# Agent attention and a gated feed-forward: attention matmuls moved to even steps, scores in one piece

## The chip, the core and the metric

The kernel runs on one core of a Trainium2 chip. The core has a matrix engine (TensorE, PE in the profile, with its weight loads as PEld), three elementwise engines (VectorE or DVE, ScalarE or ACT, GpSimd or POOL) and SyncE (SP), which here only issues DMAs. Each engine works through its own instruction queue in order and waits on semaphores of the others. The metric is the device time of one execution, in microseconds (us).

## The reference

```
q, k, v: (4, 12480, 128)   agents: (4, 49, 128)   w_in: (128, 2048)   w_out: (2048, 128)
sm(a, b)  = softmax(a @ b.T / sqrt(128))
agent_v   = sm(agents, k) @ v            # 49 x 128 per batch, over all 12480 keys
x         = sm(q, agents) @ agent_v      # 12480 x 128 per batch
h         = x @ w_in
out       = (h * sigmoid(1.702 * h)) @ w_out
```

All in float32; the kernel reaches the precision by splitting operands into parts that TensorE multiplies one after the other.

## The kernel before

The kernel folds `agent_v` into `w_in`: for each batch it computes the 49 x 2048 product `agent_v @ w_in` once (`weights_0`, `weights_1`, `weights_part`, into the tiles `wh` and `wq`), so that a query's softmax row over 49 agents is multiplied straight into the hidden layer.

Queries are worked in 52 groups of 960 tokens (13 for each of the 4 batches), in two halves of 480 columns. For each group the 2048 hidden units are 16 **steps** of 128. The main loop, `two_steps(t)`, takes two steps at a time, so 416 rounds. TensorE's work in a round is always the same:

- `up`: four matmuls of 128 rows (L407) and then **the quad** (L410), four matmuls with 19 rows each, placed in four row groups of the array. They leave four banks `ph` in PSUM;
- two calls of `down`, six matmuls of 480 columns each (L445), which add the hidden units of the steps `t - 4` and `t - 3` to `po`.

Between them ScalarE applies the gelu from `ph` to `g` (L420), `high` rounds it to `gh` (by a DMA that POOL issues, or by ACT or DVE, depending on the step), and DVE computes the rest, `gl = g - gh` (`low`, L435).

The attention work of the following groups and of the next batch is slipped in between. A table `at` maps a step number to the jobs that are issued there. **Where a job lands in a round depends on the parity of its step**: `jobs(t)`, the even step, is called behind the quad and ahead of the first `down`; `jobs(t + 1)`, the odd step, is called in `second`, between the two `down`s. `pe_steps` is the set of steps that already hold TensorE work; `pe_step(t)` returns the first free one from `t` on.

The jobs that matter here:

- **Scores** (`scores`, L186): a group of 960 keys or queries is split into three bf16 parts (`split`: four DVE pieces at L173 and L175 that write `rest`; pieces 0 and 1 belong to the first 480 tokens, 2 and 3 to the others). Then 48 small matmuls (49 columns, bf16) produce 8 tiles of scores in one PSUM bank, 24 of them (c = 0) for the first half of the tokens and 24 (c = 1) for the other. A query group has c = 0 at step 12 of its 16 and c = 1 at step 13; a key group has them at the first two free steps from a rule on.
- **`key_store`** (L228): ACT copies the bank of key scores to `score` in SBUF; then DVE updates the running maximum from the bank (`running_max`, L225).
- **`query_shift`** (L350, L352): DVE subtracts each query's maximum; it needs the whole bank.
- **`key_values`** (L284): eight matmuls of 258 columns, `exp(score)` times values, after `value_pair` (L279, L280) has written the one buffer `v_pair`.
- `key_max_1`, `key_max_2`, `weights_1` (L311 to L313), `weights_part` (L330): a few matmuls for each batch; `query_pairs` (L379, then L389 and L391) transposes the softmax rows at step 4.

SP issues the loads (`key_load`, `query_load`, `value_load`) in the order of the steps. There are two PSUM banks (`ps_m`) for all the attention work, two buffers for `rest`, one for a query group's load.

Of the kernel before, what the change touches and what calls it, by code (L numbers as in the profile page):

```python
# [18 lines left out]
TB = 120  # L19
KB = 8  # L20
# [7 lines left out]
Q_AT = 12  # L28
E_AT = 0
P_AT = 4  # L30
S_AT = 8
K_AT = 3
V_AT = (6, 11)
V_LAST = 5
R = 30
FIRST_WORDS = 1
FIRST_UP = 2
# [6 lines left out]
def kernel(  # L44
# [11 lines left out]
    B, C, N = qT.shape  # L56
    A = agT.shape[2]
    F = w_in.shape[1] // 2
    NF = F // P
    NG = N // GT  # L60
    NKG = N // (TB * KB)
# [28 lines left out]
    for i in range(2):  # L90
        t = const.tile([P, KB, P], F32R, name=f"e_pair{i}")
# [14 lines left out]
    score = const.tile([P, NKG * KB, A], F32, name="score")  # L106
# [59 lines left out]
    def split(t):  # L166
        r = work.tile([P, GT + PAD], F32, name="rest", tag="rest")
        nc.gpsimd.memset(t[:, GT:], 0.0)

        def piece(i):  # L170
            s = slice(0, CH + PAD) if i < 2 else slice(CH + PAD, GT + PAD)
            if i % 2 == 0:
                nc.vector.tensor_sub(out=r[:, s], in0=t[:, s], in1=halves(t)[0][:, s])  # L173
            else:
                nc.vector.tensor_sub(out=halves(r)[1][:, s], in0=r[:, s], in1=halves(r)[0][:, s])  # L175

        return (halves(t)[0], halves(r)[0], halves(r)[1]), piece

    def scores(b, parts, ps, c):
        x0, x1, x2 = parts  # L180
        for j in range(c * KB // 2, (c + 1) * KB // 2):
            t = slice(j * TB, j * TB + P)
            o = ps[:, j * A : (j + 1) * A]
            products = [(x0, 0), (x0, 1), (x0, 2), (x1, 0), (x1, 1), (x2, 0)]
            for i, (x, y) in enumerate(products):
                nc.tensor.matmul(  # L186
                    out=o,
                    lhsT=x[:, t],
                    rhs=ag_part[:, b, y, :],
                    start=(i == 0),  # L190
                    stop=(i == len(products) - 1),
                )

    def score_bank():
        ps = ps_m.tile([P, 512], F32, name="ps_m")
        return ps, ps[:TB, : KB * A].rearrange("p (j a) -> p j a", a=A)
# [24 lines left out]
    def running_max(g, s):  # L221
        if g == 0:
            nc.vector.tensor_copy(out=run_max[:TB], in_=s)
        else:
            nc.vector.tensor_tensor(out=run_max[:TB], in0=s, in1=run_max[:TB], op=ALU.max)  # L225

    def key_store(g, s):
        nc.scalar.copy(out=score[:TB, g * KB : (g + 1) * KB, :], in_=s)  # L228
        running_max(g, s)

    def key_max_0(d):
        mx = work.tile([P, A], F32, name="mx", bufs=1)
        nc.vector.tensor_reduce(out=mx[:TB], in_=run_max[:TB].rearrange("p j a -> p a j"), axis=AX.X, op=ALU.max)
        d["mx"] = mx
# [28 lines left out]
    def key_shift(g, sub):  # L263
        sc = score[:TB, g * KB : (g + 1) * KB, :]
        sub(out=sc, in0=sc, in1=max_b[:TB].unsqueeze(1).broadcast_to([TB, KB, A]), op=ALU.subtract)  # L265
# [5 lines left out]
    def key_pair(g):  # L271
        sc = score[:TB, g * KB : (g + 1) * KB, :]
        ep = e_pair[g % 2]
        nc.vector.tensor_copy(out=ep[:TB, :, 0:A], in_=sc)
        nc.vector.tensor_sub(out=ep[:TB, :, H : H + A], in0=sc, in1=ep[:TB, :, 0:A].bitcast(F32))
# [67 lines left out]
    def query_load(b, g):  # L343
        t = loads.tile([P, GT + PAD], F32, name="qt", tag="qt", bufs=1)
        nc.sync.dma_start(out=t[:, 0:GT], in_=qT[b, :, g * GT : (g + 1) * GT])
        return t

    def query_shift(s):
        m = work.tile([P, KB], F32, name="m")
        nc.vector.tensor_reduce(out=m[:TB], in_=s, axis=AX.X, op=ALU.max)  # L350
        sd = e_sb[:TB, :, 0:A]
        nc.vector.tensor_tensor(  # L352
            out=sd, in0=s, in1=m[:TB].unsqueeze(2).broadcast_to([TB, KB, A]), op=ALU.subtract
        )
        return sd
# [118 lines left out]
    def do_key_load(b, g):  # L474
        if b < B and g < NKG:
            kts[b, g] = key_load(b, g)
# [5 lines left out]
    def do_query_load(n):  # L482
        if n < B * NG:
            qts[n] = query_load(*divmod(n, NG))

    def do_key_split(b, g, i):
        if i == 0:
            k_parts[b, g], pieces[b, g] = split(kts.pop((b, g)))
        pieces[b, g](i)
# [7 lines left out]
    def do_key_scores(b, g, c):  # L497
        if c == 0:
            banks[b, g] = score_bank()
        scores(b, k_parts[b, g], banks[b, g][0], c)  # L500

    def do_key_store(b, g):
        key_store(g, banks.pop((b, g))[1])

    def do_key_values(b, g):
        sums[b, g] = key_values(g)
# [6 lines left out]
    def do_query_scores(n, c):  # L513
        if n < B * NG:
            if c == 0:
                banks[n] = score_bank()
            scores(n // NG, q_parts[n], banks[n][0], c)

    def do_query_shift(n):
        if n < B * NG:  # L520
            scored[n] = query_shift(banks.pop(n)[1])
# [94 lines left out]
    steps = B * NG * NF  # L616
    per_batch = NG * NF
    at = {}
    pe_steps = {n * NF + f for n in range(B * NG) for f in (Q_AT, Q_AT + 1, P_AT)}

    def put(t, fn):
        at.setdefault(t, []).append(fn)


    def pe_step(t):
        while t in pe_steps:
            t += 1
        pe_steps.add(t)
        return t
# [7 lines left out]
    for b in range(B - 1):  # L637
        s0 = b * per_batch
        done = s0
        for k in range(NKG):  # L640
            t = pe_step(s0 + (11 + 5 * k if b == 0 else K_AT + 11 * k // 2))
            t1 = pe_step(t + 1)
            put(t - 13 if b else max(t - 13, 0), lambda b=b, k=k: do_key_load(b + 1, k))
            begin = max(t - 4, done + 1)
            for i in range(4):
                put(min(begin + i, t - 1 if i < 2 else t1 - 1), lambda b=b, k=k, i=i: do_key_split(b + 1, k, i))
            done = t1
            put(t, lambda b=b, k=k: do_key_scores(b + 1, k, 0))
            put(t1, lambda b=b, k=k: do_key_scores(b + 1, k, 1))
            put(t1 + 1, lambda b=b, k=k: do_key_store(b + 1, k))  # L650
        mx = {}
        put(t1 + 2, lambda mx=mx: key_max_0(mx))
        t = pe_step(t1 + 3)
        put(t, lambda mx=mx: key_max_1(mx))
        t = pe_step(t + 2)
        put(t, lambda mx=mx: key_max_2(mx))
        shift = t + 1

        g0 = (shift + 1 - s0 - E_AT + NF - 1) // NF
        for k in range(NKG):  # L660
            slot = s0 + (g0 + k // 2) * NF + E_AT
            exps.setdefault(slot, []).append(k)
            last = k == NKG - 1
            t = slot + (V_LAST if last else V_AT[k % 2])
            put(min(shift + 3 * k, slot - 1), lambda k=k: key_shift(k, nc.vector.tensor_tensor))
            put(t - 16, lambda b=b, k=k: do_value_load(b + 1, k))
            put(t - 4, lambda b=b, k=k: value_pair(vts.pop((b + 1, k))))
            put(slot + 3 - last, lambda k=k: key_pair(k))
            assert t not in pe_steps
            put(t, lambda b=b, k=k: do_key_values(b + 1, k))  # L670
            put(t + 1, lambda b=b, k=k: do_key_sum(b + 1, k))
        w = {}
        put(t + 2, lambda b=b, w=w: weights_0(accs.pop(b + 1), w))
        t = pe_step(t + 3)
        put(t, lambda w=w: weights_1(w))
        for c in range(F // 512):
            t = pe_step(t + (3 if c else 1))
            assert t < s0 + per_batch + 4 * c - 5, (b, shift - s0, g0, t - s0)
            put(t, lambda b=b, w=w, c=c: weights_part(b + 1, w, c))
    for n in range(B * NG):  # L680
        s0 = n * NF
        if n:
            put(s0 + E_AT, lambda n=n: do_query_exp(n + 1))
            if s0 + E_AT in exps:
                ks = exps[s0 + E_AT]
                put(s0 + E_AT, lambda ks=ks: key_exp(ks[0], len(ks)))
            put(s0 + E_AT + 2, lambda n=n: do_query_sums(n + 1))
            put(s0 + E_AT + 2, lambda n=n: do_query_softmax(n + 1))
        put(s0 + P_AT, lambda n=n: do_query_pairs(n + 1))
        for i in range(4):  # L690
            put(s0 + S_AT + i, lambda n=n, i=i: do_query_split(n + 2, i))
        for c in range(2):
            put(s0 + Q_AT + c, lambda n=n, c=c: do_query_scores(n + 2, c))
        put(s0 + Q_AT + 2, lambda n=n: do_query_load(n + 3))
        put(s0 + Q_AT + 2, lambda n=n: do_query_shift(n + 2))


    E = mybir.EngineType
    g = {}
# [98 lines left out]
```

## Time and profile before

| | |
|---|---|
| median of 3 runs | 2039.23 us (2039.01 to 2040.26) |
| the profiled execution's own time | 2040.92 us |
| its span, from the first to the last instruction | 2039.1 us |
| VectorE busy | 1576.9 us (77%) |
| ScalarE busy | 1440.2 us (71%) |
| GpSimd busy | 281.4 us (14%) |
| mean share of the 16 DMA engines, by slices | 3 to 9 tenths, mostly 5 |
| granted clock of TensorE | 0.988 on average; full speed in all but the first slices |

The profiled execution is 1.69 us above the median of the runs, and its span 1.82 us below its own time. The page's busy time of TensorE counts instructions whose modelled ends overlap; what a piece of its work costs is read from the starts of what follows, in the chain of waits or in the timeline.

### The profile page before, as it was taken

To read this page: it belongs to the slowest core of one execution; us is meant where nothing else is said; L and a number is where in the kernel's file an instruction comes from. 1 tells how busy PE (TensorE), PEld (TensorE's weight loads), DVE (VectorE), ACT (ScalarE), POOL (GpSimd) and SP (SyncE) were. 2 spreads that over 40 slices of the span, in tenths; PEclk is the share of its full clock that TensorE was granted. 3 is DMA by queue.
4 is the path that set the end of the run, shared out by engine and by line. 5 is a ranking of instruction groups with operands and counts; after the bars stand their busy time and mean duration, and the time that the engine had idled before them with its cause. 6 is when DMAs were issued, how large, how long until landed. Compare 5 with 4: busy or idle time off the path is not lost.

```text
span 2039.1 us, 36417 instructions
## 1 busy us (share of the span) xinstructions
PE 1992.4 (98%) x13688; PEld 1525.2 (75%) x13688; DVE 1576.9 (77%) x2025; ACT 1440.2 (71%) x2457; POOL 281.4 (14%) x594
## 2 busy tenths in 40 slices
PE   8789999999999999999999999999999999999999
PEld 7567777777777777777777777777777777777776
DVE  4788888888777879888777888888877776767665
ACT  3256677677776777777776677777777877777775
POOL 3011111111111111111111111111111111111111
PEclk9799999999999999999999999999999999999999
DMA  9645556565455565565555555566545545455443
GB/s 252 180 157 182 180 181 184 172 190 174 159 170 174 181 191 181 173 190 175 170 172 171 180 190 175 170 191 174 170 164 161 178 156 170 155 171 165 161 157 134
DMA packets 129444, 356.00 MB, mean 175 GB/s; under 512 B 15696, under 2 KB 48688, under 8 KB 129268
## 3 DMA queue, kind: packets, MB, share of 16 engines
q0 software_dynamic: 67520, 230.22, 34.4%
q1 hardware_dynamic: 61748, 123.46, 20.9%
q8 instruction: 108, 1.77, 0.4%
q14 instruction: 68, 0.56, 0.1%
HBM read 80.97 MB, written 25.56 MB: 52 GB/s over the span
## 4 chain that ended last, share of the span: by engine, by line
PE 89%; DVE 5%; ACT 2%; DMA 2%; issue 1%; POOL 1%; SPq 0%; ACTq 0%; POOLq 0%; DVEq 0%
PE po L445 53%; PE ph L407 17%; PE ph L410 8%; PE ps_m L186 6%; PE ps_m L284 2%; DVE gl L435 1%; DMA gh<-g 1%; PE ps_m L379 1%; PE ps_m L209 1%; ACT g L420 1%; PE ps_m L330 1%; DVE rest L173 1%; DVE rest L175 1%; POOL score L265 1%; DMA words<-w_in 0%
## 5 line engine op out<-in xcount | busy, mean ns | idle before, releaser
L420 ACT ACTIVATE g<-ph 128x480 f32<-128x480 f32 x1664 | 816.6, 577 | 494.4 <-PE ph L410 489.3
L435 DVE TENSOR_TENSOR gl<-g,gh 128x960 fp32r<-128x960 f32 x832 | 941.3, 1153 | 192.5 <-DMA gh<-g 101.9
L445 PE MATMUL po<-gh,wo_h 128*128 128x480 f32 x1664 | 551.7, 413 | 1.9 <-DMA gh<-g 1.9
L445 PE MATMUL po<-gl,wo_h 128*128 128x480 f32 x1664 | 502.1, 383 | 4.9 <-DVE gl L435 4.3
L445 PE MATMUL po<-gh,wo_l 128*128 128x480 f32 x1664 | 500.2, 382 | 0.0
L426 POOL DMA_DIRECT2D gh<-g x468 | 252.0, 538 | 1689.9 <-ACT g L420 1129.2
L445 PEld LDWEIGHTS po<-gl,wo_h 128*128 128x128 f32 x1664 | 311.6, 189 | 63.0 <-DVE gl L435 14.9
L445 PEld LDWEIGHTS po<-gh,wo_l 128*128 128x128 f32 x1664 | 314.0, 189 | 49.8
L445 PEld LDWEIGHTS po<-gh,wo_h 128*128 128x128 f32 x1664 | 273.2, 189 | 85.4 <-issue 64.8
L407 PE MATMUL ph<-sa,wh 128*128 128x480 f32 x832 | 319.8, 384 | 4.8 <-ACT g L420 3.3
L407 PE MATMUL ph<-sb,wh 128*128 128x480 f32 x832 | 321.6, 386 | 0.0
L430 ACT CAST gh<-g 128x960 fp32r<-128x960 f32 x312 | 311.8, 999 | 9.0
L410 PE MATMUL ph<-rq,wq 19*128 19x480 f32 x1664 | 205.2, 481 | 0.0
L407 PEld LDWEIGHTS ph<-sa,wh 128*128 128x128 f32 x832 | 157.4, 189 | 37.4 <-ACT g L420 11.0
L407 PEld LDWEIGHTS ph<-sb,wh 128*128 128x128 f32 x832 | 157.2, 189 | 35.4 <-ACT g L420 11.6
L410 PEld LDWEIGHTS ph<-rq,wq 19*128 19x128 f32 x1664 | 80.0, 182 | 137.0 <-issue 136.5
L186 PE MATMUL ps_m<-ag_part,rest 128*128 128x49 bf16 x2184 | 130.3, 185 | 6.6 <-DVE rest L175 6.4
L175 DVE TENSOR_TENSOR rest<-rest 128x480 bf16<-128x480 f32 (+1 forms) x182 | 129.8, 719 | 0.4
L186 PEld LDWEIGHTS <-rest 128*128 128x128 bf16 x2184 | 109.4, 97 | 8.4 <-DVE rest L175 7.8
L225 DVE TENSOR_TENSOR run_max<-ps_m,run_max 120x392 f32<-120x392 f32 x36 | 20.4, 567 | 79.3 <-ACT score L228 79.1
L186 PEld LDWEIGHTS <-qt 128*128 128x128 bf16 x1248 | 61.3, 98 | 25.1 <-issue 25.0
L186 PE MATMUL ps_m<-ag_part,qt 128*128 128x49 bf16 x1248 | 74.6, 186 | 0.0
(97 smaller groups left out, 1326.8 us busy)
## 6 DMA issues: line engine op xcount, KB each, us to landing
gh<-g POOLq DMA_DIRECT2D x468, 480.0 KB, 3.6
kt<-kT SPq DMA_DIRECT2D x52, 480.0 KB
qt<-qT SPq DMA_DIRECT2D x52, 480.0 KB
vt<-v SPq DMA_DIRECT2D x52, 480.0 KB
outT<-o SPq DMA_DIRECT2D x104, 240.0 KB
rq<-sa SPq DMA_DIRECT2D x104, 35.6 KB
rq<-sb SPq DMA_DIRECT2D x104, 35.6 KB
sa<-sa SPq DMA_DIRECT2D x104, 28.1 KB
```

Source lines behind the costliest of these rows:

```text
L173: nc.vector.tensor_sub(out=r[:, s], in0=t[:, s], in1=halves(t)[0][:, s])
L175: nc.vector.tensor_sub(out=halves(r)[1][:, s], in0=r[:, s], in1=halves(r)[0][:, s])
L186: nc.tensor.matmul(out=o, lhsT=x[:, t], rhs=ag_part[:, b, y, :], start=(i == 0), stop=(i == len(products) - 1),)
L225: nc.vector.tensor_tensor(out=run_max[:TB], in0=s, in1=run_max[:TB], op=ALU.max)
L284: nc.tensor.matmul(out=ps[:, : 2 * C + 2], lhsT=e_pair[g % 2][:TB, j, :], rhs=v_pair[:TB, j, :], start=(first and j == 0), stop=(last and ...
L407: nc.tensor.matmul(out=ph[k][:, :CH], lhsT=wh[:, cols[i]], rhs=pairs[c], start=True, stop=False)
L410: nc.tensor.matmul(out=ph[k][:, :CH], lhsT=wq[r, cols[i]], rhs=rq[r], start=False, stop=True, tile_position=(k * 32, 0),)
L420: nc.scalar.activation(out=gs[i][:, c, :], in_=ph[k][:, :CH], func=AF.Gelu_apprx_sigmoid)
L426: nc.gpsimd.dma_start(out=gh, in_=g)
L430: nc.scalar.copy(out=gh, in_=g)
L435: nc.vector.tensor_sub(out=gl, in0=g, in1=gh.bitcast(F32))
L445: nc.tensor.matmul(out=po[c][:, :CH], lhsT=lhsT[:, f, :], rhs=rhs[:, c, :], start=(begin and first), stop=(end and last),)
```

## The change

All TensorE jobs of the attention are put at even steps, so behind a quad. `pe_step` returns only even steps. The two halves of a group's scores stand at the same step, one behind the other. A key group's steps are two written lists (`K_FIRST` for the keys that are scored during batch 0, `K_AT` for later batches), asserted to be free; the four split pieces all stand ahead of that step. The second value group of a slot moves from step 11 to step 10. The query's load and shift move from step 14 to step 13. The running maximum moves out of `key_store` to the step after it, and reads the stored `score` in SBUF and not the PSUM bank.

```diff
-K_AT = 3
-V_AT = (6, 11)
-V_LAST = 5
+K_FIRST = (10, 16, 22, 26, 32, 38, 42, 48, 54, 58, 62, 66, 70)
+K_AT = (6, 10, 16, 22, 26, 32, 38, 42, 48, 54, 58, 64, 70)
+V_AT = (6, 10)
...
         nc.scalar.copy(out=score[:TB, g * KB : (g + 1) * KB, :], in_=s)
-        running_max(g, s)
...
-    pe_steps = {n * NF + f for n in range(B * NG) for f in (Q_AT, Q_AT + 1, P_AT)}
+    pe_steps = {n * NF + f for n in range(B * NG) for f in (Q_AT, P_AT)}
...
-        while t in pe_steps:
+        while t % 2 or t in pe_steps:
...
-            t = pe_step(s0 + (11 + 5 * k if b == 0 else K_AT + 11 * k // 2))
-            t1 = pe_step(t + 1)
+            t = s0 + (K_AT if b else K_FIRST)[k]
+            assert pe_step(t) == t
...
-                put(min(begin + i, t - 1 if i < 2 else t1 - 1), lambda b=b, k=k, i=i: do_key_split(b + 1, k, i))
-            done = t1
-            put(t, lambda b=b, k=k: do_key_scores(b + 1, k, 0))
-            put(t1, lambda b=b, k=k: do_key_scores(b + 1, k, 1))
-            put(t1 + 1, lambda b=b, k=k: do_key_store(b + 1, k))
+                put(min(begin + i, t - 1), lambda b=b, k=k, i=i: do_key_split(b + 1, k, i))
+            done = t
+            for c in range(2):
+                put(t, lambda b=b, k=k, c=c: do_key_scores(b + 1, k, c))
+            put(t + 1, lambda b=b, k=k: do_key_store(b + 1, k))
+            put(t + 2, lambda k=k: running_max(k, score[:TB, k * KB : (k + 1) * KB, :]))
...
-            last = k == NKG - 1
-            t = slot + (V_LAST if last else V_AT[k % 2])
+            t = slot + V_AT[k % 2]
...
-            put(slot + 3 - last, lambda k=k: key_pair(k))
+            put(slot + 3, lambda k=k: key_pair(k))
...
-            put(s0 + Q_AT + c, lambda n=n, c=c: do_query_scores(n + 2, c))
-        put(s0 + Q_AT + 2, lambda n=n: do_query_load(n + 3))
-        put(s0 + Q_AT + 2, lambda n=n: do_query_shift(n + 2))
+            put(s0 + Q_AT, lambda n=n, c=c: do_query_scores(n + 2, c))
+        put(s0 + Q_AT + 1, lambda n=n: do_query_load(n + 3))
+        put(s0 + Q_AT + 1, lambda n=n: do_query_shift(n + 2))
```

Line numbers of the changed kernel behind `key_store` are one below those of before.

The first place is TensorE at steps 12 and 13 of a query group. Before, the last score matmul of the first half (from `rest`) is followed by a whole `down` of six, and then the second half begins (from `qt`):

```order
L186 LDWEIGHTS rest
L186 MATMUL ps_m<-ag_part,rest 128x49
L445 MATMUL po_872<-gh,wo_h 128x480
L445 MATMUL po_873<-gh,wo_h 128x480
L445 MATMUL po_872<-gl,wo_h 128x480
L445 MATMUL po_873<-gl,wo_h 128x480
L445 MATMUL po_872<-gh,wo_l 128x480
L445 MATMUL po_873<-gh,wo_l 128x480
L186 LDWEIGHTS qt
L186 MATMUL ps_m<-ag_part,qt 128x49
```

Now, at the same place, the second half follows the first at once:

```order
L186 LDWEIGHTS rest
L186 MATMUL ps_m<-ag_part,rest 128x49
L186 LDWEIGHTS qt
L186 MATMUL ps_m<-ag_part,qt 128x49
L186 LDWEIGHTS qt
```

The `down` that stood between the halves now stands behind all 48.

The second place is DVE at the second and third key group that is scored during batch 1 (steps 6 to 10 of that batch). `rest<-kt` are pieces of the key split, `rest<-qt` of the query split. Before, the running maximum of the first group stands directly ahead of the split of the second, reads the PSUM bank, and has the second group's pieces behind it:

```order
L435 TENSOR_TENSOR gl<-g,gh 128x960
L223 COPY run_max<-ps_m 120x392
L173 TENSOR_TENSOR rest<-kt 128x488
L435 TENSOR_TENSOR gl<-g,gh 128x960
L175 TENSOR_TENSOR rest<-rest 128x488
L435 TENSOR_TENSOR gl<-g,gh 128x960
L173 TENSOR_TENSOR rest<-kt 128x480
L175 TENSOR_TENSOR rest<-rest 128x480
L173 TENSOR_TENSOR rest<-qt 128x488
```

Now (from the changed kernel's instructions at the same group):

```order
L434 TENSOR_TENSOR gl<-g,gh 128x960 x2
L173 TENSOR_TENSOR rest<-kt 128x488
L434 TENSOR_TENSOR gl<-g,gh 128x960
L223 COPY run_max<-score 120x392
L175 TENSOR_TENSOR rest<-rest 128x488
L173 TENSOR_TENSOR rest<-qt 128x488
L434 TENSOR_TENSOR gl<-g,gh 128x960
L173 TENSOR_TENSOR rest<-kt 128x480
L175 TENSOR_TENSOR rest<-rest 128x480
```

The maximum reads `score` and stands one round later, behind the first piece of the next split.

The third place is DVE at steps 4 to 8 of a group in which values are worked. Before, the sum of the value product that TensorE has just made (`acc`, L301) stands ahead of the next writing of `v_pair`:

```order
L391 TENSOR_TENSOR sa<-ps_m,sa 49x480
L391 TENSOR_TENSOR sb<-ps_m,sb 49x480
L435 TENSOR_TENSOR gl<-g,gh 128x960 x2
L301 TENSOR_TENSOR acc<-ps_m,acc 128x257
L279 CAST v_pair<-vt 120x8x128
L280 TENSOR_TENSOR v_pair<-vt,v_pair 120x8x128
L265 TENSOR_TENSOR score<-score,max_b 120x392
L435 TENSOR_TENSOR gl<-g,gh 128x960
```

Now `v_pair` is written a step earlier, ahead of the first `gl` of the round:

```order
L390 TENSOR_TENSOR sa<-ps_m,sa 49x480
L390 TENSOR_TENSOR sb<-ps_m,sb 49x480
L434 TENSOR_TENSOR gl<-g,gh 128x960
L278 CAST v_pair<-vt 120x8x128
L279 TENSOR_TENSOR v_pair<-vt,v_pair 120x8x128
L434 TENSOR_TENSOR gl<-g,gh 128x960
L300 TENSOR_TENSOR acc<-ps_m,acc 128x257
L264 TENSOR_TENSOR score<-score,max_b 120x392
```

`v_pair` can only be written when TensorE has read its last contents, at the even step of the same round; two `gl` now stand behind that wait in place of one.

## Rows read from the trace of the kernel before

**Rows 1.** The page: span, busy time of engines, chain by engine.

```profile
span 2039.1 us, 36417 instructions
...
PE 1992.4 (98%) x13688; PEld 1525.2 (75%) x13688; DVE 1576.9 (77%) x2025; ACT 1440.2 (71%) x2457; POOL 281.4 (14%) x594
...
PE 89%; DVE 5%; ACT 2%; DMA 2%; issue 1%; POOL 1%; SPq 0%; ACTq 0%; POOLq 0%; DVEq 0%
```

**Rows 2.** Chain of waits, 900 to 960 us: start, length, engine, tile, line, matmuls.

```profile
935.83 0.87 PE ph L407 x4
...
939.95 0.87 PE ph L407 x4
...
948.17 1.45 PE ph L407 x4
...
953.24 0.87 PE ph L407 x4
...
954.54 1.15 PE ps_m L284 x8
...
958.34 0.87 PE ph L407 x4
```

**Rows 3.** Timeline of TensorE, 1000 to 1010 us: start, length, instruction, shapes, count.

```profile
1000.72 0.70 PE L445 MATMUL po<-gh,wo_h 128*128 128x480 f32 x2
...
1002.14 1.12 PE L284 MATMUL ps_m<-v_pair,e_pair 120*128 120x258 f32 x8
1003.09 0.60 PE L445 MATMUL po<-gh,wo_h 128*128 128x480 f32 x2
...
1004.41 0.38 PE L407 MATMUL ph<-sa,wh 128*128 128x480 f32 x1
...
1005.79 0.25 PE L186 MATMUL ps_m<-ag_part,qt 128*128 128x49 bf16 x3
...
1006.42 0.68 PE L445 MATMUL po<-gh,wo_h 128*128 128x480 f32 x2
...
1007.81 0.25 PE L186 MATMUL ps_m<-ag_part,qt 128*128 128x49 bf16 x3
...
1008.44 0.69 PE L445 MATMUL po<-gh,wo_h 128*128 128x480 f32 x2
...
1009.84 0.38 PE L407 MATMUL ph<-sa,wh 128*128 128x480 f32 x1
```

**Rows 4.** Who waited for whom: total us, times, longest us.

```profile
PEld ph L407 <- ACT g L420: 22.5, 70, 3.1
...
DVE m L350 <- PE ps_m L186: 13.3, 20, 2.1
...
PE ps_m L186 <- DVE rest L175: 6.4, 11, 1.0
```

**Rows 5.** Timeline of TensorE at a key group's scores, step 56; wait in brackets.

```profile
235.84 0.20 PE L186 MATMUL ps_m<-ag_part,rest 128*128 128x49 bf16 x1 [0.97 <-DVE rest L175]
```

**Rows 6.** Timeline of VectorE ahead of those scores.

```profile
232.97 0.57 DVE L225 TENSOR_TENSOR run_max<-ps_m,run_max 120x392 f32<-120x392 f32 x1 [1.64 <-ACT score L228]
```

**Rows 7.** Groups by line and shape: count, busy us, mean ns, idle before.

```profile
L445 PEld LDWEIGHTS po<-gh,wo_l 128*128 128x128 f32 x1664 | 314.0, 189 | 49.8
...
L225 DVE TENSOR_TENSOR run_max<-ps_m,run_max 120x392 f32<-120x392 f32 x36 | 20.4, 567 | 79.3 <-ACT score L228 79.1
...
L225 DVE TENSOR_TENSOR run_max<-score,run_max 120x392 f32<-120x392 f32 x12 | 6.8, 568 | 13.4 <-ACT score L218 13.4
```

**Rows 8.** Timeline of TensorE at a batch's new weights, steps 184 and 185.

```profile
1036.09 1.10 PE L330 MATMUL ps_m<-w_in_sb,avT 128*128 128x512 f32 x2 [0.48 <-DVE avT L318]
```

**Rows 9.** Timeline of VectorE at a query's shift.

```profile
934.47 0.57 DVE L350 TENSOR_REDUCE m<-ps_m 120x8 f32<-120x392 f32 x1
935.07 0.57 DVE L352 TENSOR_TENSOR e_sb<-ps_m,m 120x392 f32<-120x392 f32 x1
935.55 2.42 DVE L435 TENSOR_TENSOR gl<-g,gh 128x960 fp32r<-128x960 f32 x2
```

More of the change, by code (lines that the diff above doesn't have):

```diff
@@ L645 @@
             for i in range(4):
-                put(min(begin + i, t - 1 if i < 2 else t1 - 1), lambda b=b, k=k, i=i: do_key_split(b + 1, k, i))
-            done = t1
-            put(t, lambda b=b, k=k: do_key_scores(b + 1, k, 0))
-            put(t1, lambda b=b, k=k: do_key_scores(b + 1, k, 1))
-            put(t1 + 1, lambda b=b, k=k: do_key_store(b + 1, k))
+                put(min(begin + i, t - 1), lambda b=b, k=k, i=i: do_key_split(b + 1, k, i))
[4 more added lines that the diff above has]
+            put(t + 2, lambda k=k: running_max(k, score[:TB, k * KB : (k + 1) * KB, :]))
         mx = {}
-        put(t1 + 2, lambda mx=mx: key_max_0(mx))
-        t = pe_step(t1 + 3)
+        put(t + 2, lambda mx=mx: key_max_0(mx))
+        t = pe_step(t + 3)
         put(t, lambda mx=mx: key_max_1(mx))
```

## The prediction

> **What bounds the kernel now.** I read the page first: TensorE is busy for 98% of a span of 2039.1 us, VectorE for 77%, ScalarE for 71%, and 89% of the chain that ended last lies on TensorE [rows 1]. So the time is the sum of what TensorE's instructions cost one behind the other, plus the few waits between them. The page's mean durations overlap and can't be summed, so I went on to the chain of waits and then to TensorE's timeline, and took every piece from its start to the start of the next.
>
> In the chain a round without attention work takes 939.95 - 935.83 = 4.12 us, and one with a value product behind the quad 958.34 - 953.24 = 5.10, so 0.98 for the product [rows 2]. In the timeline [rows 3]:
>
> - a `down` behind a quad takes 1002.14 - 1000.72 = 1.42 us, one that isn't 1004.41 - 1003.09 = 1.32. The quad makes the `down` behind it 0.10 dearer;
> - a piece of 24 score matmuls takes 0.63, behind a quad (1005.79 to 1006.42) as between the `down`s (1007.81 to 1008.44);
> - the `down` behind a score piece takes 1.39 and 1.40. So a score piece makes it 0.08 dearer than 1.32, but where a quad stood ahead of the piece, the quad's 0.10 is no longer paid;
> - a value product between `down`s takes 1003.09 - 1002.14 = 0.95, with 1.32 behind it.
>
> Last I read the list of waits for what can move with the order [rows 4], and the timelines at three of these places.
>
> **The change part by part.**
>
> Scores. The piece at the even step costs 0.63 + 1.39 - 1.42 = 0.60 us, the one at the odd step 0.63 + 1.40 - 1.32 = 0.71 [rows 3]. Behind the first piece the second is left with its own 0.63, so each piece that leaves an odd step saves 0.08. The old table has 94 of them: 50 queries at step 13 (52 groups, two scored ahead of the loop) and 44 of the 78 key pieces. 94 x 0.08 = 7.5 us. That two pieces run on at one cadence isn't shown in the main loop; the bounds are 0.63 (the cadence within a piece) and 0.71 (nothing won), and I take 0.63: between the two halves stands nothing that isn't also within one.
>
> Values. 21 value products leave odd steps (in each of three batches six at step 11 and the last at step 5). Behind a quad each costs 0.98 in place of 0.95: 21 x 0.03 = +0.6.
>
> Weights and maxima. 9 weight parts and 5 transposes of the maximum also leave odd steps. No row has them at both places; by the value product such a move costs 0.03, by the score piece it wins 0.08, so between -1.1 and +0.4 for 14. I take 0, the value product being the nearer, since they too are float32 and long. `weights_1` stood one step ahead of the first weight part, so TensorE waited 0.48 us for `avT` [rows 8]; now four steps lie between, and three such waits go: -1.5.
>
> Running maximum. It costs the same from SBUF as from the bank, 568 and 567 ns [rows 7]. What goes is VectorE's wait for ScalarE's copy ahead of it, 79.1 us over 36 [rows 7]. That isn't TensorE's own wait; it reaches TensorE only where a piece of the split is late by it. One such place is step 56: VectorE has waited 1.64 us for the copy with the split pieces behind it [rows 6], and TensorE waits 0.97 us for a piece, with a few of the 24 matmuls done [rows 5]. There are 11 such waits, 6.4 us [rows 4]. By the new table all four pieces are issued at least a step ahead of the scores, and the maximum at t + 2 mostly finds the copy of t + 1 done. Bounds 0 and -6.4; I take -5, because some of these waits belong to the first rounds, where VectorE still converts weights.
>
> What is late next. The block needs pieces 2 and 3 some 0.63 us behind its start, no longer a `down` later. That is tight where a key group stands at step 6 of 16: its last piece is then at step 5, behind the operations of `query_pairs` at step 4. The two lists have 14 such groups. If none waits it costs 0; if each waits like the worst of before, 14 x 0.97 = 13.6. The mean wait of before is 6.4 / 11 = 0.6; I take that at a quarter of the groups: +2.
>
> Query shift. It waits for the block and stands ahead of a `gl` in VectorE's queue. The shift takes 0.57 + 0.57 and the `gl` half of 2.42 [rows 9], so that `gl` is there 2.35 us behind the block's end. TensorE reads it after two `down`s (1.39 + 1.32), `up` and quad (4.12 - 1.42 - 1.32 = 1.38), another `down` (1.42) and two matmuls (0.5): 6.0 us. The 3.6 us between hide the wait; without them, each group costs what it is over. The same holds for `v_pair`, which is written a step earlier and has one more `gl` behind its wait for TensorE: that delays VectorE by at most the product, 0.95. Both 0.
>
> Weight parts at step 2. The subtraction that waits for ScalarE's copy of the weights now stands ahead of the query's sums, once in each batch. Between 0 and three times the longest wait of score matmuls for VectorE, 1.0 [rows 4]; I take +0.5.
>
> Loads. Key and query loads stand up to a step elsewhere in SP's queue; what they wait for, the score block that reads their buffer, ends earlier by up to a `down`: 0. The waits of `up` for ScalarE's gelu, 22.5 us [rows 4], as in the 1.45 in place of 0.87 at 948.17 [rows 2], come from the exponentials at step 0, which stay where they are: 0.
>
> **The sum.** -7.5 + 0.6 - 1.5 - 5 + 2 + 0.5 = -10.9 us. The profiled execution took 2040.92 (its span 2039.1 and 1.82 around it), so 2030.0; it was 1.69 above the median of the runs. I predict 2028.
>
> **A rule weighed against the rows.** A 128-row weight load takes 189 ns [rows 7], and six matmuls with their loads 1.32 us, 0.22 each [rows 3]; 480 columns can't be done in the 0.03 that the load would leave, so most of a load is hidden behind the matmul before it. The Trainium skill, in "TensorE: Matmul & The Clock Gate", section "The mechanism" (Part 3), says that a weight load overlaps running matmuls only when it goes to another row group. By that rule every matmul pays for its own load wherever it stands, a place behind the quad is worth nothing, and the 7.5 us would be 0. The rows speak against it.
>
> **The rivals.**
>
> A. VectorE takes the gain back. The 14 blocks at step 6 wait 0.6 us each (8.4 in place of 2), and the waits struck out above come back at other steps (0 in place of -5): -7.5 + 0.6 - 1.5 + 8.4 + 0.5 = +0.5, so 2040, and half of that 2035 to 2037. For it: waits for VectorE already reach TensorE at the key scores [rows 4]. Against it: 79 us of VectorE's own waits go [rows 7].
>
> B. The place of a piece makes no difference, each piece pays for the change of kind. Then -7.5 is 0, and with no waits won either the time stays at 2039. Against it: the `down` behind a piece takes 1.39 with a quad ahead of the piece and 1.40 without, so the quad's 0.10 is gone in the first case [rows 3].
>
> C. Slower: the shift blocks VectorE. It waits for a block twice as long, with a `gl` behind it; before, it waited 13.3 us in 20 groups [rows 4]. It decides once VectorE's `gl` comes more than 3.6 us later than worked out above. If 50 groups are each over by 0.3 us, that is +15: 2028 + 15 = 2043; at 0.6 us, 2058. For it: VectorE's queue is in order, and in key phases a piece of a key's split stands right ahead of the shift. Against it: the 3.6 us of cover are more than three `gl`.
>
> **How the numbers follow.** The forecast gets 0.76, A 0.11, B 0.04, C 0.09. The forecast's own range goes from all of the old waits gone and no new ones (2039.2 - 7.5 + 0.6 - 1.5 - 6.4 - 1.1 = 2023, and 4 lower if VectorE's freed 79 us shorten waits that I left alone, 2019) to half of the scores' gain with the rest as taken (2032). A stretches it to 2037; C is left out: 2019 to 2037. A measurement of this kernel tells a change of 0.2%, some 4 us, from none. Faster by more: the forecast, 0.76; within it: A and B, 0.15; slower: C, 0.09.
>
> **What would show it.** In the new trace a query's round should take 5.35 us and not 5.43, no `down` that isn't behind a quad should stand behind a score piece, VectorE's maximum should hardly wait for ScalarE, nor TensorE for `avT`, and the waits of score matmuls for `rest` should be few. The forecast is wrong if the block of 48 takes 1.34 us or more, if waits for `rest` at step 6 come to over 8 us, or if TensorE waits for a `gl` behind the query's shift.

## The result and the profile after

The changed kernel takes 2018.49 us (median of 5 runs, 2017.69 to 2019.76) against 2039.23: the ratio is 0.9899, with a 95% interval of 0.9885 to 0.9914. It is 20.7 us faster. The forecast was 2028 with a range of 2019 to 2037: the sign was right, the gain was nearly twice the size, and the time lies just below the range.

The page of the profiled execution, in the lines of [rows 1]:

```profile
span 2018.0 us, 36431 instructions
...
PE 1978.4 (98%) x13688; PEld 1534.3 (76%) x13688; DVE 1584.3 (79%) x2025; ACT 1440.1 (71%) x2457; POOL 285.5 (14%) x594
...
PE 87%; DVE 4%; DMA 3%; issue 3%; ACT 2%; POOL 1%; SPq 0%; ACTq 0%; POOLq 0%; DVEq 0%
```

Nothing changed in kind: TensorE bounds the kernel, 21.1 us of span are gone. The order did what it should. This is TensorE's timeline at a query's scores in the changed kernel, to be read from start to start as [rows 3]:

```profile
916.05 0.25 PE L186 MATMUL ps_m<-ag_part,qt 128*128 128x49 bf16 x3
...
917.29 0.69 PE L444 MATMUL po<-gh,wo_h 128*128 128x480 f32 x2
...
918.70 0.60 PE L444 MATMUL po<-gh,wo_h 128*128 128x480 f32 x2
...
920.01 0.38 PE L406 MATMUL ph<-sa,wh 128*128 128x480 f32 x1
```

The block of 48 takes 1.24 us, the `down` behind it 1.41, the second `down` 1.31: 3.96 us. Before, two pieces and two `down`s took 0.63 + 1.39 + 0.63 + 1.40 = 4.05 [rows 3]. So a group saves 0.09, where 0.08 was forecast.

The waits went down too. First VectorE's own, ahead of the maximum (total in us, count, longest); then TensorE's waits for VectorE, summed for the line that waited (L186 scores, L444 `down`; total in us and count):

```profile
DVE run_max L225 <- ACT score L228: 29.6, 12, 2.9
```

```profile
  DVE rest L175: 3.2, 6
```

```profile
  DVE gl L434: 17.3, 23
```

Before, the maximum waited 79.1 us [rows 7], and the same two summaries for L186 and L445 gave:

```profile
  DVE rest L175: 14.2, 23
```

```profile
  DVE gl L435: 19.1, 38
```

The 14.2 are 6.4 us that matmuls waited [rows 4] and 7.8 that their weight loads did. A weight load and the matmul behind it can wait for the same piece, so such a total is more than TensorE lost; what it lost is summed from start to start in the part on the prediction.

### The profile page after: what moved, and what is told of

The parts are those of the page before. It is cut to its first block, busy times and chain, and to the rows that moved or that the text cites. A ratio compares the mean times of both kernels' runs of the same rounds, so it can differ in the third digit from the quotient of the medians.

```text
span 2018.0 us, 36431 instructions
## 1 busy us (share of the span) xinstructions
PE 1978.4 (98%) x13688; PEld 1534.3 (76%) x13688; DVE 1584.3 (79%) x2025; ACT 1440.1 (71%) x2457; POOL 285.5 (14%) x594
## 4 chain that ended last, share of the span: by engine, by line
PE 87%; DVE 4%; DMA 3%; issue 3%; ACT 2%; POOL 1%; SPq 0%; ACTq 0%; POOLq 0%; DVEq 0%
PE po L444 52%; PE ph L406 17%; PE ph L409 8%; PE ps_m L186 6%; DMA gh<-g 2%; PE ps_m L283 2%; DVE gl L434 1%; PE ps_m L209 1%; PE ps_m L378 1%; ACT g L419 1%; POOL score L264 1%; PE ps_m L329 0%; DMA words<-w_in 0%; POOL gh L425 0%; ACT L357 0%
## 5 line engine op out<-in xcount | busy, mean ns | idle before, releaser
L444 PE MATMUL po<-gh,wo_h 128*128 128x480 f32 x1664 | 540.6, 406 | 0.0
L444 PE MATMUL po<-gl,wo_h 128*128 128x480 f32 x1664 | 501.1, 382 | 5.7 <-DVE gl L434 5.4
L444 PE MATMUL po<-gh,wo_l 128*128 128x480 f32 x1664 | 500.0, 382 | 0.0
L425 POOL DMA_DIRECT2D gh<-g x468 | 256.5, 548 | 1659.9 <-ACT g L419 1131.7
L444 PEld LDWEIGHTS po<-gl,wo_h 128*128 128x128 f32 x1664 | 313.2, 189 | 61.3 <-DVE gl L434 11.9
L444 PEld LDWEIGHTS po<-gh,wo_l 128*128 128x128 f32 x1664 | 314.4, 189 | 50.2
L444 PEld LDWEIGHTS po<-gh,wo_h 128*128 128x128 f32 x1664 | 283.2, 189 | 82.6 <-issue 55.8
L406 PEld LDWEIGHTS ph<-sb,wh 128*128 128x128 f32 x832 | 157.0, 189 | 34.8 <-ACT g L419 11.0
L175 DVE TENSOR_TENSOR rest<-rest 128x488 bf16<-128x488 f32 (+1 forms) x182 | 129.7, 721 | 0.9
L186 PE MATMUL ps_m<-ag_part,rest 128*128 128x49 bf16 x2184 | 121.8, 185 | 1.5 <-DVE rest L175 1.5
L186 PEld LDWEIGHTS <-rest 128*128 128x128 bf16 x2184 | 109.2, 97 | 1.9 <-DVE rest L175 1.8
L186 PEld LDWEIGHTS <-qt 128*128 128x128 bf16 x1248 | 61.9, 98 | 12.8 <-issue 12.7
L186 PE MATMUL ps_m<-ag_part,qt 128*128 128x49 bf16 x1248 | 70.4, 186 | 0.0
L390 DVE TENSOR_TENSOR sa<-ps_m,sa 49x480 fp32r<-49x480 f32 x52 | 33.9, 651 | 43.6 <-ACT sb L388 43.2
```

The lines of the kernel that those rows point to most:

```text
L186: nc.tensor.matmul(out=o, lhsT=x[:, t], rhs=ag_part[:, b, y, :], start=(i == 0), stop=(i == len(products) - 1),)
L390: nc.vector.tensor_sub(out=lo[c], in0=parts[c], in1=hi[c].bitcast(F32))
L406: nc.tensor.matmul(out=ph[k][:, :CH], lhsT=wh[:, cols[i]], rhs=pairs[c], start=True, stop=False)
L425: nc.gpsimd.dma_start(out=gh, in_=g)
L444: nc.tensor.matmul(out=po[c][:, :CH], lhsT=lhsT[:, f, :], rhs=rhs[:, c, :], start=(begin and first), stop=(end and last),)
```

## The experiments

Each run was timed beside the kernel before (medians 2039.2 to 2040.1 in all comparisons). Where two changed versions are compared, I give the difference of their medians; at 4 us or less the intervals of their ratios overlap, so such a difference counts only together with what the trace shows. I had two explanations. Theory 1: VectorE's standstill ahead of the running maximum was the source of TensorE's waits. Theory 2: the earlier place of the split pieces took them away. The order was to be measured by itself.

**The order alone, for the queries.**

```diff
-            put(s0 + Q_AT + c, lambda n=n, c=c: do_query_scores(n + 2, c))
+            put(s0 + Q_AT, lambda n=n, c=c: do_query_scores(n + 2, c))
...     # load and shift at Q_AT + 1
```

> The kernel before, with only the query groups' scores in one piece behind the quad of step 12 (shift and load at 13); keys, values and maximum as before. If the gain of the order is what the rounds show (a query's round 5.42 before, 5.32 in the changed kernel), 50 x 0.10 = 5.0 us go: 2034. If the place of a piece makes no difference and the whole gain is waits of TensorE for VectorE, nothing goes: 2039. If the shift behind a block of 48 blocks VectorE, waits for gl behind it appear and it is over 2039.

2041.40, ratio 1.0007 (0.9998 to 1.0016): nothing gained. The groups without key scores do save 0.1 us each. The profile shows where it is lost: at steps 60, 220 and 428 the second half of the block waits. TensorE at step 60, and VectorE ahead of it:

```profile
247.27 0.20 PE L186 MATMUL ps_m<-ag_part,rest 128*128 128x49 bf16 x1 [1.50 <-DVE rest L175]
...
247.86 1.15 PE L445 MATMUL po<-gh,wo_h 128*128 128x480 f32 x2
```

```profile
243.25 0.57 DVE L225 TENSOR_TENSOR run_max<-ps_m,run_max 120x392 f32<-120x392 f32 x1 [2.53 <-ACT score L228]
243.73 0.66 DVE L173 TENSOR_TENSOR rest<-kt 128x488 f32<-128x488 f32 x1
244.31 0.65 DVE L173 TENSOR_TENSOR rest<-qt 128x480 f32<-128x480 f32 x1
244.88 1.15 DVE L435 TENSOR_TENSOR gl<-g,gh 128x960 fp32r<-128x960 f32 x1
245.94 1.27 DVE L175 TENSOR_TENSOR rest<-rest 128x488 bf16<-128x488 f32 x2
```

VectorE stood still for 2.53 us ahead of a maximum, so the query's last piece ended at 247.2, and the block, which now needs it a `down` earlier, waited 1.50 us. Before, the `down` between the halves had covered that.

The wait isn't the whole loss. From 247.6 to 251.0 us the granted clock of TensorE is 0.51, the lower of its two levels (1.2 GHz), and the `down` that starts at 247.86 takes 2.54 us in place of 1.39. The same happens behind the wait of 1.47 us at step 428, but not behind the one of 1.47 at step 220. The rounds of steps 60 and 428 take 2.7 us more than before, that of step 220 only 1.15. So, as an estimate from these three rounds, some 3 us of this run's loss are the clock; without them it would still be well above the 2034 of the rounds.

**The maximum alone.**

```diff
         nc.scalar.copy(out=score[:TB, g * KB : (g + 1) * KB, :], in_=s)
-        running_max(g, s)
...
+            put(t1 + 2, lambda k=k: running_max(k, score[:TB, k * KB : (k + 1) * KB, :]))
```

> The kernel before, with only the running maximum one step later and from the stored scores. Theory 1: VectorE standing still for ScalarE's copy is what made its pieces and gl late; then of the some 14 us of TensorE's waits for VectorE in the key phases that the changed kernel no longer has, most go: 2028 to 2031. Theory 2: those waits went because all four split pieces are now issued ahead of the scores' step; then 0 to 2 us go here: 2037 to 2039.

2024.00, ratio 0.9924 (0.9912 to 0.9937): -15.8 us from one moved instruction, even more than theory 1 gave it. (It also reads the stored scores and not the bank. The two were not run apart, but in the kernel before no wait of TensorE for the maximum's hold on the bank is listed.) TensorE's waits for `rest` and for `gl` in this run:

```profile
  DVE rest L175: 3.1, 4
```

```profile
  DVE gl L434: 7.2, 10
```

Both fell, 14.2 to 3.1 and 19.1 to 7.2. The second is what the prediction had not counted.

VectorE's standstill itself is by no means gone, 79.1 us before and now

```profile
DVE run_max L225 <- ACT score L228: 50.9, 28, 3.7
```

One step later a piece of the next split stands ahead of the maximum and no longer behind it. At step 64 VectorE stood still for 3.81 us before and 3.60 now; from the starts, TensorE lost 1.46 us behind it at the scores of step 66 before, and nothing now. So what counts is which work stands behind the standstill, more than how long it is.

**The split pieces alone.**

```diff
-                put(min(begin + i, t - 1 if i < 2 else t1 - 1), lambda ...: do_key_split(b + 1, k, i))
+                put(min(begin + i, t - 1), lambda ...: do_key_split(b + 1, k, i))
```

> The kernel before, with only the third and fourth split piece of a key group issued ahead of the step of the first scores. Theory 1 (the maximum's wait is the cause): 0 to -2 us, 2037 to 2039. Theory 2 (the place of the pieces is the cause): the waits of score matmuls for rest go, -7 us or more: 2032 or less.

2036.76, ratio 0.9986 (0.9977 to 0.9994): -3.0, more than theory 1 said and less than half of what theory 2 needs. It helps a little; it isn't the cause.

**The maximum put back into the changed kernel.**

```diff
+        running_max(g, s)
...
-            put(t + 2, lambda k=k: running_max(k, score[:TB, k * KB : (k + 1) * KB, :]))
```

> The changed kernel with the running maximum back beside ScalarE's copy, from the bank. Theory 1: VectorE's waits for the copy are back (79 us in all) and TensorE's waits with them, up to +8: 2022 to 2027. Theory 2: the pieces are early, so TensorE sees little of it: 2018 to 2020.

2021.39, ratio 0.9911 (0.9898 to 0.9925): +2.9 on the changed kernel, between the two theories. With the pieces early, most of the standstill is covered. What isn't covered shows at the places that the prediction had named, the 14 key groups at step 6:

```profile
PEld L186 <- DVE rest L175: 4.5, 14, 0.6
```

**Order of the queries and maximum together** (both diffs above).

> The kernel before, with two parts of the change: the query groups' scores in one piece behind the quad, and the running maximum one step later from the stored scores. Theory 1 (alone, the order saves 0.10 us a query group, but the block then waits for split pieces that stand behind VectorE's blocked maximum): with the maximum out of the way the block finds its pieces, so the full 50 x 0.10 = 5 us come on top of the maximum's part alone (2024.0): 2018 to 2020. Rival (the block of 48 meets late pieces whatever the maximum does): no gain on top of 2024, 2023 to 2026.

2020.22, ratio 0.9905 (0.9892 to 0.9919): 3.8 us below the maximum alone. The order gains nothing by itself, and near to what its rounds say (5) once VectorE isn't blocked. These two parts of the change alone come within 1.7 us of the changed kernel.

**All blocks between the `down`s.**

```diff
-                put(t, lambda b=b, k=k, c=c: do_key_scores(b + 1, k, c))
+                put(t + 1, lambda b=b, k=k, c=c: do_key_scores(b + 1, k, c))
...     # queries at Q_AT + 1; what follows one step later
```

> The changed kernel with all 89 score blocks moved from behind the quad of their round to between its two downs (all that follows them one step later). Theory: a down behind a quad is 0.10 us dearer than one that isn't, and a block behind the quad takes that over; between the downs the quad's 0.10 is paid as well as the block's: 89 x 0.10 = +8.9, less up to 2 for pieces that have half a round more: 2025 to 2028. Rival (what counts is that the scores are one piece and not two): 2017 to 2020.

2026.79, ratio 0.9936 (0.9924 to 0.9949): +8.3. The timeline of TensorE at a query's scores, with the `down` now ahead of the block:

```profile
920.52 0.71 PE L444 MATMUL po<-gh,wo_h 128*128 128x480 f32 x2
...
921.94 0.25 PE L186 MATMUL ps_m<-ag_part,qt 128*128 128x49 bf16 x3
...
923.18 0.68 PE L444 MATMUL po<-gh,wo_h 128*128 128x480 f32 x2
...
924.58 0.38 PE L406 MATMUL ph<-sa,wh 128*128 128x480 f32 x1
```

1.42 + 1.24 + 1.40 = 4.06 us, against 3.96 behind the quad and 4.05 in two pieces. Making one piece of two gains nothing; the place behind the quad does.

**The weight parts off step 2.**

```diff
-            t = pe_step(t + (3 if c else 1))
+            t = pe_step(t + (6 if c == 1 else 3 if c else 1))
```

> The changed kernel with the weight parts of a batch at steps 190, 198, 202 and 206 of the batch and not 190, 194, 198 and 202, so that none stands at step 2 of a group, where VectorE's subtraction waits for ScalarE ahead of the query's sums. Theory: TensorE's 0.66 + 0.27 + 0.32 us of waits at step 4 of the next round in each batch are due to it and go: -3.7, so 2015. Rival (they come from ScalarE's exponentials at step 0, as in other groups): 2018.

2015.32, ratio 0.9883 (0.9868 to 0.9898): -3.2 on the changed kernel, the expected size. VectorE in the changed kernel at step 194 of a batch:

```profile
1044.31 0.68 DVE L332 TENSOR_TENSOR wl<-ps_m,wh 49x512 fp32r<-49x512 f32 x1 [5.15 <-ACT wh L330]
...
1045.74 0.57 DVE L367 TENSOR_TENSOR p_pad<-e_sb,z 120x392 f32<-120x392 f32 x1
```

TensorE's transposes need `p_pad` and waited for it:

```profile
1046.37 0.63 PE L378 MATMUL ps_m<-ident,p_pad 120*128 120x120 f32 x4 [0.59 <-DVE p_pad L367]
```

From start to start the transposes come 0.66 us late in each of the three batches, and in this run they don't. But the theory also had the waits for `gl` in the same rounds go, and these stay: 1.7 us over the three batches in the changed kernel, 1.8 here. So the path is shown for 2.0 of the 3.2 us; another 1.0 went at step 202 of batch 0, and that the sum is right is in part luck.

**The second value product behind the quad of step 0.**

```diff
-V_AT = (6, 10)
+V_AT = (6, 16)
```

> The changed kernel with the second value product of a slot behind the quad of step 0 of the next group and not at step 10. Theory: the up of step 4 waits some 0.6 us in each group with key exponentials because the rounds of steps 0 and 2 are shorter than ScalarE's work in them; a product of 1 us put there lengthens them and the wait goes, at no cost, since the product is only moved: 18 x 0.6 = -10.8, so 2008. Rival (ScalarE starts that much later too and the wait stays, or VectorE's pairs are late for the product): 2016 to 2020.

2008.15, ratio 0.9844 (0.9831 to 0.9857): -10.3. The wait of `up` for ScalarE, 22.5 us in 70 places before [rows 4] and 21.7 in 67 after, is now

```profile
PEld ph L406 <- ACT g L419: 8.8, 17, 3.1
```

and in the chain the product stands behind the quad of step 0, with the `up` of step 4 at its plain 0.87, where [rows 2] have 1.45:

```profile
881.53 1.15 PE ps_m L283 x8
...
889.41 0.87 PE ph L406 x4
...
890.71 0.56 PE ps_m L378 x4
```

**Both of these.**

> The changed kernel with both of the last two edits: weight parts at steps 190, 198, 202 and 206, the second value product of a slot at step 16. They lie in different stretches (the last two groups of a batch, the groups with key exponentials), so their gains should add up: 2018.5 - 3.2 - 10.3 = 2005. Rival (the longer rounds of step 0 had already given the weight parts' waits their time, or the other way round): one of the two alone, 2008.

2005.27, ratio 0.9829 (0.9816 to 0.9842): the gains add up, 34.8 us below the kernel before. This version beats both kernels.

**The query load a step later, in that version.**

> The kernel of the last run (weight parts and values moved) with only the query load back from step 13 to step 14. In the runs where the load was moved to 13 the DMA that makes gh landed later and VectorE waited longer for it (100 to 160 us in all, against 97 to 105 in the runs with the load at 14). Theory: the load's 480 KB share the DMA engines with the gh of step 12; at 14 they don't, and VectorE's waits for gh fall back to about 100 us, while the time falls by 0 to 3 us (2002 to 2005), since most of these waits were covered. Rival (the waits are longer only because VectorE comes earlier): they stay at 140 or more and the time at 2005.

2004.79, ratio 0.9827 (0.9813 to 0.9840): no difference from the last run, and VectorE's waits for the DMA hardly fall, from 152.6 to

```profile
DVE gl L434 <- DMA gh<-g: 143.8, 122, 4.3
```

The theory falls: it isn't the load's place that makes `gh` land later (a median of 4.1 us from issue to landing in both).

## Why the prediction was wrong

**What failed is the step on the running maximum.** It named the right mechanism and gave it 0 to -6.4 us, and -5 as its value. By itself it is worth -15.8, and in the whole change the waits of this kind that went were worth 14.0 (the balance below). Two mistakes are in that bound.

It took the list's 6.4 us for all that TensorE loses to late pieces. The row counts from the modelled end of the matmul before, while the round loses from start to start. At step 56 the row says 0.97 [rows 5]; the first score matmul of that piece and the `down` behind it, in the kernel before, are

```profile
234.58 0.25 PE L186 MATMUL ps_m<-ag_part,kt 128*128 128x49 bf16 x3
...
236.34 0.68 PE L445 MATMUL po<-gh,wo_h 128*128 128x480 f32 x2
```

So the piece takes 1.76 us in place of 0.63, and 1.13 are lost. The second piece of the same group waits again. Summed over all pieces from the starts, in excess of their usual time, it is 9.6 us before, 2.1 with the maximum alone moved and 2.2 after.

And it let VectorE's standstill reach TensorE only through `rest`. VectorE's queue is one line: what stands behind a blocked maximum is late, the `gl` for a `down` as much as a piece. These waits stand mostly on the weight loads, in another row of the list than those of the matmuls (kernel before; the longest of each is in the first rounds):

```profile
PEld po L445 <- DVE gl L435: 14.9, 34, 3.4
...
PE po L445 <- DVE gl L435: 4.3, 4, 3.0
```

The prediction counted neither. Summed from the starts, and leaving out the first rounds, such waits cost 6.6 us before in the rounds in which a key group is worked (5.6 of them at `down`s, 1.0 at the transposes of step 4) and 0.5 with the maximum alone moved.

**Point by point.** Scores: 94 x 0.08 = 7.5 was forecast. By the rows a piece saves 0.09, and the run with the blocks between the `down`s costs 8.3 / 89 = 0.09 for each, so some 8.5: right, a little small. Values, 0.03 each: too small to be seen in a run. `avT`: its three waits are gone as forecast, and from the starts each was worth 0.65. Step 6: 2 us of new waits forecast at 14 groups; the 2.2 that are left stand all at such groups, 2.0 of it at three, and all 14 wait once the maximum blocks again. Weight parts at step 2: +0.5 forecast; in the changed kernel the rounds behind them lose 2.0 us at the transposes, which the run with the parts moved took away, and 1.7 at `down`s, whose cause it leaves open. I had bounded it by a score piece's wait, but VectorE waits 5.15 us for ScalarE there, with all of a query's sums behind it. Query shift: no wait of TensorE for a `gl` behind it.

One gain was in no term. At step 202 of batch 0 TensorE waited for a `gh` that a DMA brought late. Its waits for such DMAs in the whole run, before (a load's and a matmul's, both for this `gh`) and after (three loads, one at this step):

```profile
  DMA gh<-g: 4.3, 2
```

```profile
  DMA gh<-g: 1.0, 3
```

From the starts the rounds of steps 202 and 204 lost 4.3 us before and 1.0 after. A part of the 4.3 is the clock again: from 584.4 to 587.8 us it is granted at 0.50, so behind its first slices the kernel before did not run at full speed everywhere.

The balance, summed from the starts over the main loop, in us:

| term | forecast | shown |
|---|---|---|
| order of scores, values, weights and maxima | -7.5 + 0.6 | -8.5 |
| wait for `avT` | -1.5 | -1.9 |
| waits for split pieces, the old and the new | -5 + 2 | -7.4 |
| waits for `gl` and at the transposes, where a key group is worked | none | -6.6 |
| the same behind the weight parts | +0.5 | +3.7 |
| late `gh` at step 202 | none | -3.3 |
| waits for `gl` at step 4 of five other groups | none | +3.3 |
| first rounds, and all `up`s | none | +0.4 |

The last column gives -20.3; the main loop took 21.3 us less, and 1.0 is too scattered to be placed. So the waits for VectorE that went were worth 11.0 us more than forecast, the order and `avT` 2.0 more. Waits that were forecast too low or not at all took 6.9 back, and 3.3 came as a gain that nobody had forecast. That the last two partly cancel, so that the time lies only just below the range, is luck.

None of the prediction's three signs of being wrong came: the block takes 1.24 us, the waits for `rest` at step 6 come to 2.2, and no `gl` behind the shift is waited for. They looked for new losses, and the miss lay in the size of the old ones. VectorE's maximum, which should hardly wait, still waits 29.6 us, nearly without harm.

**The rivals.** A came in part: 14.0 us of waits went, but 7.0 appeared at other steps, at the weight parts and at step 4. Its mechanism is also what the first run shows, where the order alone lost its gain to VectorE. B is refuted by the 8.3 us of the run with the blocks between the `down`s. C did not come. The 8.3 us also speak against the rule of the Trainium skill ("TensorE: Matmul & The Clock Gate", "The mechanism") that the prediction weighed: by it the place behind the quad would be worth nothing.

**What stays open.** The gains aren't additive: the maximum is worth 15.8 alone and 2.9 at the end. I can't say how the 12.9 between are shared between order and early pieces. With the maximum put back, the score pieces lose 6.1 us and not 2.2, but no `gl` is late again in the rounds of the key groups, so the new places cover these by themselves. The late `gh` at step 202 cost 3.5 to 5.6 us in all runs that keep the weight parts' old places, and 1.1 or less in those with the new ones; what delayed that DMA wasn't isolated. Nor was the cause of the new waits for `gl` at step 4.

## What to carry to other kernels

On an engine with one queue in order, look at what stands behind an instruction that waits, and not only at how long the engine works: VectorE had 23% to spare, and moving one instruction that stood still behind another engine's copy was worth more than all of the rearranged matmuls. A tighter order on the bounding engine takes slack away from its suppliers, so free these first, or the gain turns into waits, as in the run with the queries alone. Sum what the waits cost from the starts of the work: a list of waits can show one wait twice, or only a part of it. And when a wait repeats at one step, a piece of work moved into that round from elsewhere can hide it at no cost.

## What the runs showed of the hardware that was not expected

Of two orders of the same matmuls the cheaper is the one in which two costly changes of kind fall together: a quad makes the next `down` 0.10 us dearer, a score block 0.08, and both in a row 0.09, not 0.18. And the DMA that makes `gh` landed after a median of 4.7 us in the changed kernel, against 3.6 before and 3.6 with the blocks between the `down`s; most of it was covered, and the last run shows that the query load's place doesn't explain it. And a wait of TensorE can cost more than its length: behind two waits of 1.50 and 1.47 us the granted clock fell to 0.5 for a stretch in which a `down` took 2.54 us in place of 1.39, while behind another of 1.47 it stayed at 1.00.
